# Moving token loads, first taps, one output sum and the halves of a sum in a convolution and mixture-of-experts kernel

## The chip, the core and the metric

The kernel runs on one core of one Trainium2 chip. The metric is the device time of one execution in microseconds (us), as the median over runs. Engines are named as in the profile: PE is TensorE (PEld its weight loader), DVE is VectorE, ACT is ScalarE, POOL is GpSimd, SP is SyncE, which here only issues DMAs. "L434" is line 434 of the kernel.

## The reference

Two stages follow each other. The first is a causal convolution over the sequence with seven taps, whose weights are the softmax of `weight` over the taps, one set for each of eight heads of 24 channels. The second sends each token to one of eight experts.

```python
# x (8, 3584, 192), weight (8, 7), w_gate (192, 8), w_local (192, 1),
# w1 (8, 192, 1024), w2 (8, 1024, 192), all float32
x[b, s, h, :] = sum_k softmax(weight[h])[k] * x_padded[b, s + k, h, :]      # 24 channels a head
logits = x @ w_gate
gate = sigmoid(x @ w_local)
e[b, s] = argmax(logits[b, s]) if s == 0 or gate[b, s] < 0.5 else e[b, s - 1]
p = softmax(logits[b, s])
out[b, s] = p[e] * (relu(x[b, s] @ w1[e]) @ w2[e])
```

There are 28,672 tokens.

## The kernel before

**Parts and blocks.** The tokens come in 16 parts of 1792. Each part is loaded, convolved, routed (expert, probability and a slot number for each token), and scattered row by row into slots in DRAM, where tokens of one expert stand together. The slots are then worked through in blocks of one expert each: blocks 0 to 27 hold one unit of 128 tokens, blocks 28 to 70 two units, then come 23 large blocks of four units (`FIRST` is 71, the first of them), then four blocks of two and 15 of one, and two that run only where they are needed. Routing and computing overlap: while TensorE works through blocks of tokens that are routed, the other engines convolve and route the parts that follow.

**One block** of the first 71 is: turn the tokens (`turn`, L402 on TensorE for one unit), the product with w1 (`hidden`, L1069, into four banks of PSUM named `hps`), ReLU on ScalarE (L1078), the product with w2 (`output`, L1090, into two banks named `yps`), and the output sum. The tokens' and the hidden units' halves are computed apart (64 of the 128 rows of TensorE's array each), so a result stands in two banks: ScalarE scales one of them by the probability into `o_sb` (L1100) and VectorE adds the other (L1104, the "output sum" below). This frees the two banks of `yps` for the next block. Last, GpSimd scatters the rows to the output (`deliver`, L1118).

**Convolution.** `conv(g)` works in six channel groups (`DQ`). For each, ScalarE multiplies by tap 0 (L424) and VectorE adds taps 1 to 6, one instruction each (L434, "steps" below). Only at the start of its fourth group (`b == DQ // 2`, three sixths) does it issue the load of the next part's tokens (L432, `load_x`, L150: one DMA of 1920 KB into one of two buffers). When a part is convolved, `logits` multiplies it on TensorE (L624), into the same `hps` banks, and ScalarE copies the logits out (L629).

**The order of the work** is written by hand, and every engine runs its instructions in that order. Between the pieces of a block stand calls of `step(time)`, which put so much of the convolution or of the routing into VectorE's queue: the generators yield the cost of what they issued, and `step` stops when the time is used up. In a block of one unit there are three such places: `step(2.1)` ahead of `output` (L1489; 2.4 at block 0), `step(1.2)` inside it between ScalarE's half and the output sum (L1102; nothing at block 0), and `step(1.3)` behind it (L1498). `st["block"]` is the number of the block, `TURNED` is 28, the first block of two units.

**Queues.** SyncE issues all loads, one after another: rows of a block from the slots (L990 for one unit, L998 and L1003 later; it waits there until the scatters of the group that fills them are done), the weights of a block (L982, 1536 KB, 512 KB chunks for the first few; four buffers, issued three blocks ahead) and the tokens (L150). GpSimd issues the scatters into the slots (`put`, L838). Where a route's logits are awaited (`st["due"]`), `output` issues none of them.

**Large blocks.** `seven` computes the hidden units of a block of four units with seven products in place of eight. Each product is a call of `times` (L1237, four matmuls, each of which the trace records twice), partial sums stand in three pairs of banks (`xb`, `wbk`, `yb`), and VectorE adds them to copies in SBUF: h22 takes `xb` (L1257), h11 takes `wbk` (L1259), h12 takes `yb` (L1269). Then come the ReLUs (L1261 for h11, in two halves) and `output_late` (L1287), which needs the ReLU of h11 for its weights. One matmul of the product `times(wbk, a13, b31)` is held back behind the next product:

```python
        put(times(xb, s3, t3))
        nc.vector.tensor_tensor(h22, xb, h22, op=Alu.add)       # L1257
        times(wbk, a13, b31, at=((1, 1),))
        nc.vector.tensor_tensor(h11, wbk, h11, op=Alu.add)      # L1259
```

Of the kernel before, what the change touches and what calls it, by code (L numbers as in the profile page):

```python
# [10 lines left out]
Act = mybir.ActivationFunctionType  # L11
Alu = mybir.AluOpType
# [5 lines left out]
P = 128  # L18
# [8 lines left out]
NPART = N // PT  # L27
# [19 lines left out]
EARLY = 3  # L47
# [46 lines left out]
DQ = D // Q  # L94
# [17 lines left out]
def kernel(  # L112
# [11 lines left out]
    nc = tc.nc  # L124
# [11 lines left out]
    op = ctx.enter_context(tc.tile_pool(name="op", bufs=2))  # L136
# [29 lines left out]
    c = cst.tile([P, DQ, KC], F32, name="c")  # L166
# [229 lines left out]
    def halves():  # L396
        return [(half, slice(half * DR, (half + 1) * DR)) for half in range(2)]
# [16 lines left out]
    def conv(g, x_sb):  # L414
        z = (z_tile() if g % 2 else
             ys[2].tile([P, NB, DG], F32, name="y_sb").rearrange("p b d -> p (b d)"))
        z = z[:, :NT * D].rearrange("p (b s) -> p b s", b=DQ)
        got[g] = z

        def chans(b, k):  # L420
            return x_sb[:, b, k * Q:(k + NT) * Q]

        def first(b):
            nc.scalar.activation(z[:, b, :], chans(b, 0), Act.Copy, scale=c[:, b, 0:1])  # L424

        first(0)
        yield 0
        for b in range(DQ):
            if b + 1 < DQ:
                first(b + 1)  # L430
            if b == DQ // 2 and 2 < g < NPART - 1:
                x_in[g + 1] = load_x(g + 1)  # L432
            for k in range(1, KC):
                nc.vector.scalar_tensor_tensor(z[:, b, :], chans(b, k), c[:, b, k:k + 1],  # L434
                                               z[:, b, :], Alu.mult, Alu.add)
                yield 0.68
# [389 lines left out]
    to_put = []  # L826
# [254 lines left out]
    def output(n, wb, xg, hT, w2):  # L1081

        yps = [yps_p.tile([P, 512], F32, name="yps") for half in range(2)]
        spots = {1: {(0, 0, 1): 0} if st["block"] and not st["due"] else {},
                 2: {(0, 0, 0): 0, (0, 1, 1): 2, (2, 0, 7): 0}}[n]
        for m4 in ([0, 1, 4, 5], [2, 3, 6, 7]):
            for k in range(n):
                for m in m4:
                    for half, rows in halves():
                        ins = nc.tensor.matmul(yps[half][:, k * D:(k + 1) * D],  # L1090
                                               lhsT=hT[rows, m, k * P:(k + 1) * P],
                                               rhs=wb[rows, w2 + m * D:w2 + (m + 1) * D],
                                               start=(m == 0 and k == 0), stop=(m == FK - 1),
                                               skip_group_check=True)
                    if len(to_put) > spots.get((m4[0], k, m), len(to_put)):
                        put(ins)
        o_sb = op.tile([P, KT, D], F32, name="o_sb")
        y = [[yps[half][:, k * D:(k + 1) * D] for half in range(2)] for k in range(n)]
        for k in range(n):
            nc.scalar.activation(o_sb[:, k, :], y[k][0], Act.Copy, scale=xg[:, k, 0:1])  # L1100

        step(1.2 if n > 1 or st["block"] else 0)  # L1102
        for k in range(n):
            nc.vector.scalar_tensor_tensor(o_sb[:, k, :], y[k][1], xg[:, k, 0:1], o_sb[:, k, :],  # L1104
                                           Alu.mult, Alu.add)

            st["hot"] = n == 1 and st["due"]
            if k == 0 and not st["hot"]:
                deliver(o_sb[:, 0, :], xg, 0)
            else:  # L1110
                held.append(lambda ins, k=k: deliver(o_sb[:, k, :], xg, k, ins))
# [108 lines left out]
    def seven(wb, wt, weight_then, xT, xc, rows_then, weights_next):  # L1220
# [10 lines left out]
            "p h (j s) -> p h j s", j=2)  # L1231
            for pool, name in ((late_p[0], "ps"), (xps_p, "xps"), (late_p[1], "ps"))]

        def times(to, a, b, first=False, at=((0, 0), (0, 1), (1, 0), (1, 1))):
            for j, half in at:
                rows = halves()[half][1]
                ins = nc.tensor.matmul(to[:, half, j, :], lhsT=b[rows, j * P:(j + 1) * P],  # L1237
                                       rhs=a[rows, :], start=(first and j == 0), stop=True,
                                       skip_group_check=True)
            return ins  # L1240

        weight_then(times(xb, a11, b11, True))
# [7 lines left out]
        times(xb, s2, t2)  # L1250
        nc.scalar.copy(h12, xb)
        put(times(wbk, a12, b21, True))
        times(wbk, a13, b31, at=((0, 0), (0, 1), (1, 0)))
        if st["block"] > FIRST:
            step(SIDE[0], early=1)
        put(times(xb, s3, t3))
        nc.vector.tensor_tensor(h22, xb, h22, op=Alu.add)  # L1257
        times(wbk, a13, b31, at=((1, 1),))
        nc.vector.tensor_tensor(h11, wbk, h11, op=Alu.add)  # L1259
        for side in range(2):  # L1260
            nc.scalar.activation(h11[:, side], h11[:, side], Act.Relu)  # L1261
        times(yb, s4, b22)
        put(times(yb, s5, b32))
        times(xb, a22, t4)
# [196 lines left out]
    for i, (_, n, _, _) in enumerate(blocks):  # L1461
# [15 lines left out]
        if i < FIRST:  # L1477
# [6 lines left out]
            else:  # L1484
# [1 line left out]
                xT = turn_late(n_next, xgs[i + 1][0])  # L1486
                xc = combine_x(xT)
                next(xc)
            step(2.4 if i == 0 else 2.1 if n == 1 else 4.2 if i < FIRST - 1 else 3.0)  # L1489
            xg = xgs.pop(i)  # L1490
            output(n, wbs.pop(i), xg if i < TURNED else xg[1], hT, w2)
            if i == 0:
# [2 lines left out]
                more_room()  # L1495
                xc = next(xc)
            if i < FIRST - 1:
                step(1.3 if n == 1 else 3.4)  # L1498
            continue
        if i == FIRST:  # L1500
            banks.close()
# [143 lines left out]
```

## Time and profile before

| what | value |
|---|---|
| three runs | 1310.39, 1309.5, 1309.29 us; median 1309.5 |
| the profiled execution | 1310.8 us, of which the span of instructions is 1309.0 |
| mean granted clock of TensorE | 0.993 |
| VectorE busy | 949.3 us (73%) |
| ScalarE busy | 541.3 us (41%) |
| GpSimd busy | 558.0 us (43%) |
| DMA | 299.6 MB, 229 GB/s over the span |

The share of the span says how long an engine was busy, not whether anything waited for it. A wait row gives for one engine and one kind of instruction what released it last, with the total idle time, how often, and the mean. A timeline row gives start, length, engine, line and instruction, runs of equal instructions as one with their count, and in square brackets the idle time just before with its releaser. A clock below 1.00 in a stretch means that TensorE was granted that share of full speed there. Block 2 begins its first product at 60.2 us, block 21 at 180.9, block 31 at 265.1; the first large block's products begin at 698.6 and the last one's end at about 1168 us.

### The profile page before, as it was taken

The page shows a single profiled execution, that of the slowest core. Times are in us where ns is not written, and L with a number is a line of the kernel's source. Part 1 is how long each engine was busy: PE and PEld are TensorE (multiplying, and loading weights), DVE is VectorE, ACT ScalarE, POOL GpSimd, SP SyncE. Part 2 cuts the span into 40 slices and gives each one's busy share as a digit, 9 for nine tenths or more (in the row PEclk, how much of TensorE's full clock was granted, in tenths as well). Part 3 has the DMA queues.
Part 4 walks back from the last instruction along what each step waited for, and adds up shares of the span by engine and source line. Part 5 has one row for each costly group of instructions (what it writes and reads, how often), then busy time and mean ns, then how long its engine had stood idle before and what let it go on. Part 6 is the DMA issues. An engine that isn't in the chain of part 4 may idle for free.

```text
span 1309.0 us, 39518 instructions
## 1 busy us (share of the span) xinstructions
PE 1273.4 (97%) x15406; PEld 1214.3 (93%) x15406; DVE 949.3 (73%) x2481; ACT 541.3 (41%) x1208; POOL 558.0 (43%) x619
## 2 busy tenths in 40 slices
PE   9899999899999999999999999999999999999997
PEld 7789999899999999999999998999999999999997
DVE  5978889799988989999888989976875434341111
ACT  5435554234343442434435444544434434342332
POOL 4444444344344444444545455355356433321221
PEclk9989999899999999999999999999999999999999
DMA  5789998988887878878787646464555635535894
GB/s 197 267 319 403 356 360 263 346 266 279 263 289 234 283 241 278 276 234 285 263 259 228 171 119 180 104 168 146 139 170 141 179 104 152 150 97 191 271 323 160
DMA packets 182675, 299.59 MB, mean 229 GB/s; under 512 B 145872, under 2 KB 157191, under 8 KB 166738
## 3 DMA queue, kind: packets, MB, share of 16 engines
q1 hardware_dynamic: 160160, 251.79, 60.3%
q0 software_dynamic: 22320, 45.22, 10.5%
q8 instruction: 123, 2.02, 0.6%
q14 instruction: 70, 0.57, 0.1%
q10 hardware_dynamic: 2, 0.00, 0.0%
HBM read 251.35 MB, written 46.07 MB: 227 GB/s over the span
## 4 chain that ended last, share of the span: by engine, by line
PE 89%; DVE 5%; issue 2%; ACT 2%; DMA 1%; POOL 0%; POOLq 0%; DVEq 0%; another core or an unknown queue 0%; ACTq 0%
PE hps L1069 23%; PE yps L1090 23%; PE ps L1287 22%; PE ps L1237 11%; PE ps L1182 5%; PE xps L1237 2%; PE hps L624 2%; DMA x_sb<-in_x_dram 1%; DVE z L434 1%; ACT hot L1261 1%; DVE hot L1257 1%; DVE hot L1259 1%; PE hps L252 1%; PE hps L189 0%; DVE hot L597 0%
## 5 line engine op out<-in xcount | busy, mean ns | idle before, releaser
L1118 POOL DMA_INDIRECT out_dram<-o_sb,head x201 | 208.7, 1038 | 454.1 <-DVE o_sb L1302 273.2
L1069 PE MATMUL hps<-xT,wb 64*128 64x256 f32 (+1 forms) x3408 | 323.0, 339 | 8.6 <-ACT ls L629 4.4
L1090 PE MATMUL yps<-wb,hT 64*128 64x192 f32 x3648 | 318.5, 326 | 3.9 <-DVE o_sb L1104 3.0
L1069 PEld LDWEIGHTS hps<-xT,wb 64*128 64x128 f32 x3408 | 289.0, 189 | 31.5 <-issue 6.9
L1090 PEld LDWEIGHTS yps<-wb,hT 64*128 64x128 f32 x3648 | 305.3, 188 | 7.5 <-DVE o_sb L1104 3.6
L1287 PE MATMUL ps<-wb,hot 64*128 64x192 f32 x3680 | 309.4, 324 | 3.0 <-ACT hot L1261 0.9
L1287 PEld LDWEIGHTS ps<-wb,hot 64*128 64x128 f32 x3680 | 299.3, 187 | 12.0 <-ACT hot L1261 10.6
L838 POOL DMA_INDIRECT slots<-y_sb,posi x228 | 232.9, 1022 | 175.1 <-PE yps L1090 87.3
L1078 ACT ACTIVATE hT<-hps 128x512 f32<-128x512 f32 (+1 forms) x284 | 130.6, 510 | 150.2 <-PE hps L1069 126.9
L434 DVE SCALAR_TENSOR_TENSOR y_sb<-x_sb,c,y_sb 128x448 f32<-128x448 f32 x252 | 172.7, 696 | 25.8 <-ACT y_sb L424 19.8
L434 DVE SCALAR_TENSOR_TENSOR z<-x_sb,c,z 128x448 f32<-128x448 f32 x252 | 173.1, 696 | 16.6 <-ACT z L424 8.6
L1302 DVE SCALAR_TENSOR_TENSOR o_sb<-ps,head,o_sb 128x192 f32<-128x192 f32 x115 | 43.2, 412 | 141.4 <-ACT o_sb L1297 138.7
L1297 ACT ACTIVATE o_sb<-ps,head 128x192 f32<-128x192 f32 x115 | 42.9, 417 | 204.7 <-PE ps L1287 182.9
L1100 ACT ACTIVATE o_sb<-yps,head 128x192 f32<-128x192 f32 x86 | 31.4, 417 | 159.0 <-PE yps L1090 81.9
L1237 PE MATMUL ps<-xT,wb 64*128 64x256 f32 x736 | 91.8, 376 | 0.0
L1161 DVE STREAM_TRANSPOSE xT<-y_sb 128x768 f32<-128x768 f32 (+1 forms) x65 | 54.9, 871 | 46.0 <-PE ps L1182 33.0
L1237 PEld LDWEIGHTS ps<-xT,wb 64*128 64x128 f32 x736 | 79.8, 187 | 2.1
L1257 DVE TENSOR_TENSOR hot<-ps,hot 128x1024 f32<-128x1024 f32 x23 | 28.2, 1224 | 65.1 <-PE ps L1237 49.2
L1182 PE MATMUL ps<-xT,wb 64*128 64x128 f32 (+1 forms) x912 | 64.2, 294 | 0.0
L1261 ACT ACTIVATE hot<-hot 128x512 f32<-128x512 f32 x46 | 26.5, 622 | 89.5 <-DVE hot L1259 73.4
L1182 PEld LDWEIGHTS ps<-xT,wb 64*128 64x128 f32 x912 | 62.7, 188 | 0.0
L1118 POOL DMA_INDIRECT out_dram<-o_sb,xg x28 | 30.3, 1083 | 75.6 <-DVE o_sb L1104 51.9
(296 smaller groups left out, 1439.6 us busy)
## 6 DMA issues: line engine op xcount, KB each, us to landing
wb<-in_w_dram SPq DMA_DIRECT2D x109, 1536.0 KB
x_sb<-in_x_dram SPq DMA_DIRECT2D x14, 1920.0 KB
y_sb<-slots SPq DMA_DIRECT2D x92, 192.0 KB
hot<-slots SPq DMA_DIRECT2D x172, 96.0 KB
wb<-in_w_dram SPq DMA_DIRECT2D x12, 512.0 KB
slots<-y_sb,posi POOLq DMA_INDIRECT x228
out_dram<-o_sb,head POOLq DMA_INDIRECT x201
x_sb<-in_xb_dram SPq DMA_DIRECT2D x4, 768.0 KB
```

What stands on the lines that cost most here:

```text
L434: nc.vector.scalar_tensor_tensor(z[:, b, :], chans(b, k), c[:, b, k:k + 1], z[:, b, :], Alu.mult, Alu.add)
L838: ins = nc.gpsimd.indirect_dma_start(out=slots[:, :], in_=rows, in_offset=None, out_offset=bass.IndirectOffsetOnAxis(ap=to, axis=0)).ins
L1069: ins = nc.tensor.matmul(hps[half][:, j, w], lhsT=wb[rows, w1 + f0:w1 + f0 + P], rhs=xT[rows, d, w], start=(d == 0 and j == 0), stop=(d == ...
L1078: nc.scalar.activation(hT[:, m:m + 2, w], hps[half][:, :, w], Act.Relu)
L1090: ins = nc.tensor.matmul(yps[half][:, k * D:(k + 1) * D], lhsT=hT[rows, m, k * P:(k + 1) * P], rhs=wb[rows, w2 + m * D:w2 + (m + 1) * D], ...
L1118: sent = nc.gpsimd.indirect_dma_start(out=out, in_=o, in_offset=None, out_offset=bass.IndirectOffsetOnAxis(ap=xg.bitcast(I32)[:, k, 1:2], ...
L1161: nc.vector.transpose(xT.rearrange("p d (j t) -> p j d t", t=Q)[:, js], rows[:, js].rearrange("p j (d t) -> p j d t", t=Q))
L1182: nc.tensor.matmul(hps[:, half, j, :], lhsT=wb[rows, f0:f0 + P], rhs=xT[rows, d, :], start=(d == 0 and j == 0), stop=(d == KD - 1), skip_g ...
L1237: ins = nc.tensor.matmul(to[:, half, j, :], lhsT=b[rows, j * P:(j + 1) * P], rhs=a[rows, :], start=(first and j == 0), stop=True, skip_gro ...
L1287: ins = nc.tensor.matmul(yps[:, half, k * D:(k + 1) * D], lhsT=h[two][rows, side, j, k * P:(k + 1) * P], rhs=wb[rows, f * D:(f + 1) * D], ...
L1297: nc.scalar.activation(o_sb[:, k, :], yps[:, 0, k * D:(k + 1) * D], Act.Copy, scale=xg[:, at + k, 0:1])
L1302: nc.vector.scalar_tensor_tensor(o_sb[:, k, :], yps[:, 1, k * D:(k + 1) * D], xg[:, at + k, 0:1], o_sb[:, k, :], Alu.mult, Alu.add)
```

## The change

Five edits, each an order of instructions; no instruction of arithmetic is added except that one sum of a large block becomes two of half its width.

- **Token loads at two sixths.** `conv(g)` issues the next part's load at the start of its second group of channels (`b == 1`), when the taps of one group are queued, in place of its fourth.
- **First taps follow ReLUs.** In blocks 1 to 27 a group no longer issues ScalarE's tap 0 of the group behind it ahead of its own steps; before each `step` ahead of `output`, `firsts(2)` issues tap 0 for up to two groups ahead, behind the ReLUs of that block.
- **Scatters.** `output` of a one-unit block now issues a scatter also while a route is due, if the next one in line belongs to part 3 (`EARLY`).
- **The second block's output sum.** In block 1 `step(2.1)` and `step(1.2)` become nothing and `step(1.3)` becomes `step(3.4)`: the convolution steps that stood ahead of and around its output sum go behind it.
- **One sum in two halves.** In `seven`, the sum of h11 is made in two halves of 512 columns; the first now stands ahead of the sum of h22, each half's ReLU behind it, and the product into `wbk` is no longer split.

```diff
@@ conv
-        first(0)
+        at = {"b": 0, "first": 0}
+
+        def firsts(more):
+            while at["first"] <= min(at["b"] + more, DQ - 1):
+                b = at["first"]
+                nc.scalar.activation(z[:, b, :], chans(b, 0), Act.Copy, scale=c[:, b, 0:1])
+                at["first"] += 1
+
+        st["firsts"] = firsts
+        firsts(0)
         yield 0
         for b in range(DQ):
-            if b + 1 < DQ:
-                first(b + 1)
-            if b == DQ // 2 and 2 < g < NPART - 1:
+            at["b"] = b
+            firsts(0 if 0 < st["block"] < TURNED else 1)
+            if b == 1 and 2 < g < NPART - 1:
                 x_in[g + 1] = load_x(g + 1)
@@ output
-        spots = {1: {(0, 0, 1): 0} if st["block"] and not st["due"] else {},
+        away = st["due"] and not (to_put and to_put[0][0] == EARLY)
+        spots = {1: {(0, 0, 1): 0} if st["block"] and not away else {},
@@
-        step(1.2 if n > 1 or st["block"] else 0)
+        step(1.2 if n > 1 or st["block"] > 1 else 0)
@@ seven
         put(times(wbk, a12, b21, True))
-        times(wbk, a13, b31, at=((0, 0), (0, 1), (1, 0)))
+        times(wbk, a13, b31)
         if st["block"] > FIRST:
             step(SIDE[0], early=1)
         put(times(xb, s3, t3))
-        nc.vector.tensor_tensor(h22, xb, h22, op=Alu.add)
-        times(wbk, a13, b31, at=((1, 1),))
-        nc.vector.tensor_tensor(h11, wbk, h11, op=Alu.add)
         for side in range(2):
+            nc.vector.tensor_tensor(h11[:, side], wbk[:, side], h11[:, side], op=Alu.add)
             nc.scalar.activation(h11[:, side], h11[:, side], Act.Relu)
+            if side == 0:
+                nc.vector.tensor_tensor(h22, xb, h22, op=Alu.add)
@@ the loop over blocks
-            step(2.4 if i == 0 else 2.1 if n == 1 else 4.2 if i < FIRST - 1 else 3.0)
+            if st["cgen"] and i < TURNED:
+                st["firsts"](2)
+            step((2.4, 0)[i] if i < 2 else 2.1 if n == 1 else 4.2 if i < FIRST - 1 else 3.0)
@@
-                step(1.3 if n == 1 else 3.4)
+                step(1.3 if n == 1 and i != 1 else 3.4)
```

Lines behind the first edit move down by four to eleven: steps from L434 to L440, the output sum from L1104 to L1111, weights from L982 to L988, rows from L990 to L996.

**VectorE, from the end of the early routing to block 4.** `y_sb_705` is the convolution of part 2 (the steps), `o_sb` the output of blocks 1, 2, 3 and so on (the output sums). Before:

```order
L915 CAST tabi0_2_905<-tab0_244 128x2
L918 TENSOR_TENSOR new_883<-ends0_250 128x8
L920 SCALAR_TENSOR_TENSOR used_242<-new_883,used_242 128x8
L434 SCALAR_TENSOR_TENSOR y_sb_705<-x_sb_393,c_117,y_sb_705 128x448 x8
L1104 SCALAR_TENSOR_TENSOR o_sb_991<-yps_972,xg_744,o_sb_991 128x192
L434 SCALAR_TENSOR_TENSOR y_sb_705<-x_sb_393,c_117,y_sb_705 128x448 x8
L1104 SCALAR_TENSOR_TENSOR o_sb_1083<-yps_1064,xg_795,o_sb_1083 128x192
```

And in the changed kernel:

```order
L921 CAST tabi0_2_906<-tab0_244 128x2
L924 TENSOR_TENSOR new_884<-ends0_250 128x8
L926 SCALAR_TENSOR_TENSOR used_242<-new_884,used_242 128x8
L440 SCALAR_TENSOR_TENSOR y_sb_705<-x_sb_393,c_117,y_sb_705 128x448 x2
L1111 SCALAR_TENSOR_TENSOR o_sb_988<-yps_969,xg_744,o_sb_988 128x192
L440 SCALAR_TENSOR_TENSOR y_sb_705<-x_sb_393,c_117,y_sb_705 128x448 x11
L1111 SCALAR_TENSOR_TENSOR o_sb_1079<-yps_1060,xg_795,o_sb_1079 128x192
L440 SCALAR_TENSOR_TENSOR y_sb_705<-x_sb_393,c_117,y_sb_705 128x448 x8
```

Ahead of block 1's output sum two steps stand in place of eight; ahead of block 2's stand eleven in place of eight, and block 3's keeps its eight.

**SyncE, around the rows of block 21.** `x_sb` is a token load, `wb` a block's weights, `xg` its rows. Before:

```order
L982 DMA wb_2640<-in_w12_dram 128x3072
...
L990 DMA xg_2750<-slots_113 128x195
...
L982 DMA wb_2755<-in_w12_dram 128x3072
...
L990 DMA xg_2842<-slots_113 128x195
...
L982 DMA wb_2847<-in_w12_dram 128x3072
L150 DMA x_sb_2922<-in_x_dram 128x3840
```

And in the changed kernel:

```order
L988 DMA wb_2639<-in_w12_dram 128x3072
...
L988 DMA wb_2749<-in_w12_dram 128x3072
L150 DMA x_sb_2795<-in_x_dram 128x3840
...
L996 DMA xg_2834<-slots_113 128x195
...
L996 DMA xg_2839<-slots_113 128x195
```

`wb_2755` and `wb_2749` are the weights of block 21, `xg_2750` and `xg_2834` its rows: they stood ahead of the weights, and now stand behind the weights and the tokens of part 5.

**SyncE, around the load of part 6's tokens.** `head` ends the rows of a block of two units. Before:

```order
L982 DMA wb_3626<-in_w12_dram 128x3072
...
L1003 DMA head_3726<-slots_113 128x2x2
...
L982 DMA wb_3735<-in_w12_dram 128x3072
...
L1003 DMA head_3813<-slots_113 128x2x2
...
L982 DMA wb_3822<-in_w12_dram 128x3072
L150 DMA x_sb_3861<-in_x_dram 128x3840
```

And in the changed kernel:

```order
L988 DMA wb_3627<-in_w12_dram 128x3072
L150 DMA x_sb_3721<-in_x_dram 128x3840
...
L1009 DMA head_3728<-slots_113 128x2x2
...
L988 DMA wb_3737<-in_w12_dram 128x3072
...
L1009 DMA head_3815<-slots_113 128x2x2
```

The tokens stood behind the weights of block 31 (`wb_3822`) and now stand behind those of block 29 (`wb_3626`, `wb_3627`): two blocks earlier in the queue, with the loads of blocks 30 and 31 behind them.

More of the change, by code (lines that the diff above doesn't have):

```diff
@@ L421, in chans @@
             return x_sb[:, b, k * Q:(k + NT) * Q]
-        def first(b):
-            nc.scalar.activation(z[:, b, :], chans(b, 0), Act.Copy, scale=c[:, b, 0:1])
-        first(0)
+        at = {"b": 0, "first": 0}
[6 more added lines that the diff above has]
+        firsts(0)
         yield 0
         for b in range(DQ):
-            if b + 1 < DQ:
-                first(b + 1)
-            if b == DQ // 2 and 2 < g < NPART - 1:
+            at["b"] = b
+            firsts(0 if 0 < st["block"] < TURNED else 1)
+            if b == 1 and 2 < g < NPART - 1:
                 x_in[g + 1] = load_x(g + 1)
@@ L1232, in seven, with times @@
             for pool, name in ((late_p[0], "ps"), (xps_p, "xps"), (late_p[1], "ps"))]
[L1234 to L1239, printed above, removed]
+        def times(to, a, b, first=False):
+            for j in range(2):
+                for half, rows in halves():
+                    ins = nc.tensor.matmul(to[:, half, j, :], lhsT=b[rows, j * P:(j + 1) * P],
+                                           rhs=a[rows, :], start=(first and j == 0), stop=True,
+                                           skip_group_check=True)
             return ins
```

## The prediction

> **What bounds the kernel now.** I read the page first, then the waits of TensorE and of its weight loader, then the timeline around each long wait. The page gives the frame.
>
> ```profile
> span 1309.0 us, 39518 instructions
> PE 1273.4 (97%) x15406; PEld 1214.3 (93%) x15406; DVE 949.3 (73%) x2481; ACT 541.3 (41%) x1208; POOL 558.0 (43%) x619
> PE 89%; DVE 5%; issue 2%; ACT 2%; DMA 1%; POOL 0%; POOLq 0%; DVEq 0%; another core or an unknown queue 0%; ACTq 0%
> ```
>
> TensorE is busy 1273.4 of 1309.0 us and holds 89% of the chain that ended last. The change removes none of its instructions, so all it can win lies in the 35.6 us in which TensorE is idle, and in stretches where it runs at half clock. The list of waits names the three largest that the change can reach.
>
> ```profile
> PEld ps L1287 <- ACT hot L1261: 10.6, 22, 0.6
> ...
> PE hps L1069 <- ACT ls L629: 4.4, 1, 4.4
> ...
> PE yps L1090 <- DVE o_sb L1104: 3.0, 1, 3.0
> ```
>
> Two are single stalls, one comes once in a large block. The single ones cost more than their length. In the table of stretches the columns are length, busy time of PE, PEld, DVE, ACT and POOL with counts, the granted clock, DMA share and GB/s.
>
> ```profile
> 62.10:65.50 3.40, 1.43 (x24) 1.14 (x20) 3.26 (x6) 3.23 (x10) 0.00 (x0) 1.00 1.06 417
> 65.52:72.34 6.82, 5.83 (x39) 5.83 (x41) 6.49 (x12) 0.42 (x1) 3.40 (x3) 0.50 1.00 413
> ...
> 249.80:253.20 3.40, 0.17 (x2) 0.00 (x0) 0.00 (x0) 0.26 (x1) 0.00 (x0) 1.00 1.16 265
> 253.26:260.07 6.81, 5.71 (x27) 5.71 (x29) 6.38 (x12) 2.39 (x7) 1.97 (x2) 0.50 1.11 300
> ```
>
> Behind each stall the clock is 0.50 for 6.8 us. TensorE works 5.83 and 5.71 us of these at half speed, so 2.9 us are lost each time on top of the wait.
>
> **Second block's output sum.** The timeline around the first stall (start, length, engine, line, instruction):
>
> ```profile
> 60.66 5.47 DVE L434 SCALAR_TENSOR_TENSOR y_sb<-x_sb,c,y_sb 128x448 f32<-128x448 f32 x8
> 61.64 0.42 ACT L1100 ACTIVATE o_sb<-yps,xg 128x192 f32<-128x192 f32 x1 [1.94 <-PE hps L1069]
> 62.97 0.56 PE L1090 MATMUL yps<-wb,hT 64*128 64x192 f32 x2
> 66.05 0.41 DVE L1104 SCALAR_TENSOR_TENSOR o_sb<-yps,xg,o_sb 128x192 f32<-128x192 f32 x1
> 66.37 5.60 DVE L434 SCALAR_TENSOR_TENSOR y_sb<-x_sb,c,y_sb 128x448 f32<-128x448 f32 x8
> 66.51 5.16 PE L1090 MATMUL yps<-wb,hT 64*128 64x192 f32 x29 [2.98 <-DVE o_sb L1104]
> ...
> 74.85 2.91 PE L1090 MATMUL yps<-wb,hT 64*128 64x192 f32 x30
> ```
>
> Block 1's output sum (L1104) frees the bank that block 2's output needs. It stands behind eight convolution steps of 0.684 us. After the change two stand ahead of it: they end at 60.66 + 1.37 = 62.03, ScalarE's half is there at 62.06, and the sum ends at 62.5, before TensorE asks at 62.97. The stall and its half clock go.
>
> What is late next is the sum of block 2. The order puts eleven steps ahead of it: 62.5 + 11 x 0.70 (5.60 / 8) + 0.41 = 70.6. Undisturbed, a block's two products take 2.68 and 2.66 us:
>
> ```profile
> 104.18 2.70 PE hps L1069 x48
> 107.00 2.66 PE yps L1090 x32
> ```
>
> So TensorE would ask at 62.97 + 2.66 + 2.70 + 0.1 = 68.4 and, one product on, idle for about 2.0 us, until 70.7. In the trace of before that place, block 3's output, is at 74.85. The gain is 4.1, and as block 3's sum (eight steps on, 70.6 + 5.60 + 0.41 = 76.6) is again some 0.3 late for block 4, I take 3.8. Bounds: 6.1 (stall and half clock, nothing late) and 0 (the new stall as long and as cold).
>
> The clock at this new stall is open. In the row of 62.10:65.50 an idle time of 1.97 of 3.40 us was enough for half clock behind it. My stall is as long, and whether so much of it falls into one such stretch depends on where the stretch begins. If it does, another 2.9 us go. [...]
>
> **Token loads at two sixths.** Around the second stall:
>
> ```profile
> 225.55 0.36 SPq L982 DMA_DIRECT2D wb<-in_w_dram  x1
> ...
> 237.20 0.38 SPq L150 DMA_DIRECT2D x_sb<-in_x_dram  x1
> ...
> 252.94 1.23 ACT L424 ACTIVATE y_sb<-x_sb,c 128x448 f32<-128x448 f32 x2 [6.56 <-DMA x_sb<-in_x_dram]
> ...
> 254.37 5.65 PE L1069 MATMUL hps<-xT,wb 64*128 64x256 f32 x24 [4.39 <-ACT ls L629]
> ```
>
> The chain of waits has the load itself, from issue to landing:
>
> ```profile
> 237.20 15.71 DMA x_sb<-in_x_dram
> ```
>
> ScalarE's first tap waits for the tokens; behind it in ScalarE's queue stands the copy of the logits, and TensorE waits for its banks. In the order the load moves from behind block 31's weights to behind block 29's (225.55), 11.3 us earlier. With the same 15.7 us it lands at 241.6; ScalarE asks at 252.94 - 6.56 = 246.4. So 4.8 us of margin, and the stall (4.4) and the cold stretch behind it (2.85) go, 7.2 in all. The weights of block 30, which the load now precedes, come later by one load; I take 7.0. Bounds: 7.2, and 0 if the queue holds the load up by as much as it was moved.
>
> An earlier load moves the other way. Here the row loads of block 21 and the order of SyncE meet:
>
> ```profile
> 55.00:200.00 145.00, 139.05 (x2208) 133.60 (x2207) 123.61 (x349) 74.68 (x232) 65.37 (x63) 0.98 0.92 354
> ...
> 165.00:170.00 5.00, 4.79 (x71) 4.66 (x70) 4.58 (x17) 3.27 (x10) 2.02 (x3) 1.00 0.36 119
> ```
>
> ```profile
> 158.43 0.33 SPq L982 DMA_DIRECT2D wb<-in_w_dram  x1
> 168.14 0.01 SPq L990 DMA_DIRECT2D xg<-slots  x1
> 168.91 0.33 SPq L982 DMA_DIRECT2D wb<-in_w_dram  x1
> ```
>
> ```profile
> 178.13 0.22 PE L402 MATMUL xps<-ident,xg 64*128 64x64 f32 x1
> ```
>
> Before, SyncE waits until 168.14 for the scatters of that group, then fetches block 21's rows, then its weights. After, weights and tokens go ahead of the rows, from about 164, when the buffer is free. At 354 GB/s weights (1536 KB) and tokens (1920 KB) take 4.4 + 5.6 us: the rows land near 178, when TensorE wants to turn them (178.13). Against that stands the stretch at 119 GB/s, where the queue had room. I book a loss of 0.7; bounds 0 and 5.6 (all of the token load). [...]
>
> The ten later loads move the same bytes into stages where TensorE waits for no transfer: nothing.
>
> **First taps behind ReLUs; scatters.** In the one-unit blocks ScalarE's taps no longer stand ahead of the ReLUs. What TensorE waited there:
>
> ```profile
> PE yps L1090 <- ACT hT L1078: 0.3, 1, 0.3
> ```
>
> I take 0.3; bounds 0.9 and -0.7 (one tap of 0.66 us in front of a copy that frees a bank). The scatters that now go while a route is due shift by one block on GpSimd, 43% busy: nothing.
>
> **Large blocks.** One block's end (timeline):
>
> ```profile
> 1042.41 1.23 DVE L1257 TENSOR_TENSOR hot<-ps,hot 128x1024 f32<-128x1024 f32 x1 [4.59 <-PE ps L1237]
> ...
> 1043.55 1.22 DVE L1259 TENSOR_TENSOR hot<-xps,hot 128x1024 f32<-128x1024 f32 x1
> ...
> 1044.68 1.22 DVE L1269 TENSOR_TENSOR hot<-ps,hot 128x1024 f32<-128x1024 f32 x1
> ...
> 1046.02 10.40 PEld L1287 LDWEIGHTS ps<-wb,hot 64*128 64x128 f32 x128 [0.46 <-ACT hot L1261]
> 1046.05 10.67 PE L1287 MATMUL ps<-wb,hot 64*128 64x192 f32 x128
> ```
>
> Three sums run back to back on VectorE; the third, which frees the bank of the output, ends at 1045.90, and the weight load starts at 1046.02. A load usually leads its product by about 0.2 us (here 0.03), so of the 0.46 some 0.25 reach TensorE. After the change half of the second sum runs ahead of the first, in VectorE's 4.59 us of idle time. A half costs about 0.70 by the nearest row of that width:
>
> ```profile
> L597 DVE TENSOR_TENSOR hot<-rel,wb 112x512 f32<-112x512 f32 x8 | 5.1, 695 | 0.0
> ```
>
> The third sum then starts about 0.4 earlier (1.22 + 0.70 in place of 2 x 1.22, and it now waits for its product), and the output goes straight on. VectorE is free at that place in 20 of 23 blocks:
>
> ```profile
> DVE hot L1257 <- PE ps L1237: 49.2, 14, 4.6
> ...
> DVE hot L1257 <- PE xps L1237: 15.7, 6, 4.0
> ```
>
> 20 x 0.25 = 5.0, less 0.1 in each of the other three, where the half delays the rest: 4.7. Bounds: 9.2 (20 x 0.46) and -3.
>
> **Sum.** 3.8 + 7.0 - 0.7 + 0.3 + 4.7 = 15.1 us. The profiled execution took 1310.8 (span 1309.0 and 1.8 around it): 1295.7. The median of the runs shown is 1.3 lower: 1294.4.
>
> **Rivals.** (1) The new stall at block 3 brings half clock again: 2.9 less, 1297.3. For it: 1.97 us of idle time were enough before. Against: it needs the stall to lie in one stretch. (2) The half sums bring nothing, because the half that now stands first delays the sum behind it and with it the next product: 4.7 less, 1299.1. The half can begin when the second sum's matmuls are done, and four others (one product) then run before the sum behind it can begin. In the chain 32 records, two to a matmul, took 3.45 us, so four matmuls take 0.9; the rival holds if a half costs more, and the 0.70 speaks against it.
>
> ```profile
> 1036.28 3.45 PE ps L1237 x32
> ```
>
> (3) The token load doesn't land in time after all and half of the 7.0 stays: 1297.9; the margin of 4.8 us speaks against it. (4) Slower: the token load ahead of rows and weights in SyncE's one queue stops TensorE in the early stage. Three loads move there (the ones that serve parts 4, 5 and 6). If each holds its next block up for all of its 5.6 us and leaves a cold stretch of 2.9, 25.5 us go and 1294.4 becomes 1319.2, less the 0.7 booked. It is slower than before from (15.1 + 0.7 + 2.6) / 3 = 6.1 us a place on. Against it: no wait of TensorE before names a transfer, and weights are issued three blocks ahead.
>
> **How the numbers follow.** Chances: forecast 0.45, (1) 0.28, (2) 0.12, (3) 0.10, (4) 0.05. The range goes from 1289.5 (no loss at block 21, all of 6.1 in block 2) to 1301.5, which takes in (1), (2), (3) and (1) with (2). Three runs spread by 1.1 us, so 0.2% or 2.6 us is about what can be told from no change; faster means under 1306.9. Only (4), or several losses together, leaves that: faster 0.94, same 0.03, slower 0.03.
>
> **What would show it.** Right: no wait of L1090 in block 2, one of about 2 us in block 3; no wait of ScalarE for tokens near 246, and full clock from there; the loader's waits at the large blocks' output gone, the stretch from one large block's output to the next shorter by 0.25; at most a short wait when block 21's rows are turned. Wrong: half clock after 68, a longer period of the large blocks, or TensorE waiting for rows or weights between 110 and 260.

## The result and the profile after

The changed kernel takes 0.9906 of the time before (95% interval 0.9891 to 0.9920): 12.3 us less on the 1309.5 us of the first runs (10.5 to 14.3), where 15.1 were forecast. The medians are 1299.7 and 1313.3 us, of 18 runs each. The profiled execution took 1300.1 us, with a span of 1298.3, 10.7 us under that of before.

```profile
span 1298.3 us, 39551 instructions
PE 1263.3 (97%) x15406; PEld 1206.5 (93%) x15406; DVE 952.3 (73%) x2504; ACT 545.5 (42%) x1208; POOL 558.1 (43%) x619
```

The waits of TensorE, and of its weight loader at the large blocks' output (the third figure of a wait row is the longest wait, not the mean):

```profile
PE xps L402 <- DMA xg<-slots: 2.7, 1, 2.7
PE yps L1097 <- DVE o_sb L1111: 2.7, 4, 1.3
...
PEld ps L1294 <- issue: 2.5, 6, 0.7
```

The stalls of 4.4 and 3.0 us and the loader's 10.6 us are gone. In their place stand a wait for rows, 2.7 us at one block, and four short ones for an output sum. Where the time went shows when the starts of blocks are set side by side (first row of L1069, now L1075, of a block in the timeline; us from one to the next). The second pair of columns is from two later executions, side by side on one chip, of the kernel before and of the changed one. Single executions differ by some us: in five later ones with the large blocks of the change, the last stretch took 625.6 to 631.3 us.

```
stretch                    before   after   less    before   after   less   forecast
start to block 4            77.54   73.44    4.1     75.27   73.31    2.0    3.8
block 4 to 28              147.14  153.91   -6.8    147.00  150.56   -3.6   -0.4
block 28 to 31              40.38   33.28    7.1     40.30   32.97    7.3    7.0
block 31 to 69             410.45  411.07   -0.6    411.61  411.23    0.4    0
block 69 to the end        633.49  626.60    6.9    635.22  625.63    9.6    4.7
span                      1309.0  1298.3    10.7   1309.4  1293.7   15.7   15.1
```

The two edits that were to gain most did so, the large blocks gained more than forecast, and the stretch from block 4 to 28 gave much of it back.

**Block 2 and 3.** The timeline of the changed kernel (start, length, engine, line, instruction; idle time before it in brackets):

```profile
61.01 1.27 DVE L440 SCALAR_TENSOR_TENSOR y_sb<-x_sb,c,y_sb 128x448 f32<-128x448 f32 x2
62.12 0.42 ACT L1107 ACTIVATE o_sb<-yps,xg 128x192 f32<-128x192 f32 x1
62.57 0.42 DVE L1111 SCALAR_TENSOR_TENSOR o_sb<-yps,xg,o_sb 128x192 f32<-128x192 f32 x1 [0.29 <-ACT o_sb L1107]
...
69.18 0.54 PE L1097 MATMUL yps<-wb,hT 64*128 64x192 f32 x2
...
70.58 0.41 DVE L1111 SCALAR_TENSOR_TENSOR o_sb<-yps,xg,o_sb 128x192 f32<-128x192 f32 x1
70.91 5.60 DVE L440 SCALAR_TENSOR_TENSOR y_sb<-x_sb,c,y_sb 128x448 f32<-128x448 f32 x8
71.05 2.70 PE L1097 MATMUL yps<-wb,hT 64*128 64x192 f32 x29 [1.33 <-DVE o_sb L1111]
```

Block 1's sum ends at 62.99, and block 2's output goes on without a wait. Block 2's sum, behind eleven steps, ends at 70.99 and stops TensorE for 1.33 us.

**The load of part 6's tokens** is issued at 228.36, and where TensorE stood for 4.39 us the logits are now followed at once by the next block at full clock (windows: length, busy time of PE, PEld, DVE, ACT and POOL, clock, DMA share, GB/s):

```profile
246.00:254.40 8.40, 8.33 (x166) 7.22 (x164) 8.15 (x14) 3.36 (x8) 2.63 (x4) 1.00 1.10 333
```

**The rows of block 21.** SyncE's DMAs, GpSimd's scatters and the turning of the rows:

```profile
164.14 1.30 SPq L150 DMA_DIRECT2D x_sb<-in_x_dram  x1
166.20 1.15 POOL L844 DMA_INDIRECT slots<-y_sb,posi  x1 [0.71 <-PE yps L1097]
...
175.01 1.25 SPq L996 DMA_DIRECT2D xg<-slots  x2
...
179.29 0.34 PE L402 MATMUL xps<-ident,xg 64*128 64x64 f32 x4 [2.74 <-DMA xg<-slots]
```

The scatter at 166.20 is the last of part 2, which SyncE waits for ahead of these rows. Before, the last one was issued at 164.01 and the rows at 168.14, in time:

```profile
164.01 0.96 POOL L838 DMA_INDIRECT slots<-y_sb,posi  x1 [0.30 <-issue]
168.14 0.01 SPq L990 DMA_DIRECT2D xg<-slots  x1
```

Now the rows are issued at 175.01 and TensorE has them at 179.29, 2.74 us late.

**Large blocks.** VectorE's three sums and the output:

```profile
1034.27 0.69 DVE L1265 TENSOR_TENSOR hot<-xps,hot 128x512 f32<-128x512 f32 x1 [3.74 <-PE xps L1244]
...
1035.13 1.23 DVE L1268 TENSOR_TENSOR hot<-ps,hot 128x1024 f32<-128x1024 f32 x1 [0.17 <-PE ps L1244]
1036.27 0.68 DVE L1265 TENSOR_TENSOR hot<-xps,hot 128x512 f32<-128x512 f32 x1
...
1036.87 1.22 DVE L1276 TENSOR_TENSOR hot<-ps,hot 128x1024 f32<-128x1024 f32 x1
...
1038.30 1.01 PE L1294 MATMUL ps<-wb,hot 64*128 64x192 f32 x10
...
1058.22 0.49 PE L1294 MATMUL ps<-wb,hot 64*128 64x192 f32 x3
```

The first half (0.69 us, forecast 0.70) is done before the sum of h22 begins, and the output no longer waits. From one output to the next it is 19.92 us, against 20.44 before (from 1046.05 to the next output, in the chain of the kernel before): 0.52 less, where 0.25 was forecast.

```profile
1066.48 10.67 PE ps L1287 x128
```

### The profile page after: what moved, and what is told of

Read it like the earlier page. It is cut to its first block, busy times and chain, and to the rows that moved or that the text cites. A ratio compares the mean times of both kernels' runs of the same rounds, so it can differ in the third digit from the quotient of the medians.

```text
span 1298.3 us, 39551 instructions
## 1 busy us (share of the span) xinstructions
PE 1263.3 (97%) x15406; PEld 1206.5 (93%) x15406; DVE 952.3 (73%) x2504; ACT 545.5 (42%) x1208; POOL 558.1 (43%) x619
## 3 DMA queue, kind: packets, MB, share of 16 engines
q0 software_dynamic: 22320, 45.22, 10.7%
## 5 line engine op out<-in xcount | busy, mean ns | idle before, releaser
L1075 PE MATMUL hps<-xT,wb 64*128 64x256 f32 (+1 forms) x3408 | 317.7, 337 | 4.7 <-issue 3.2
L1097 PEld LDWEIGHTS yps<-wb,hT 64*128 64x128 f32 x3648 | 301.6, 187 | 8.9 <-DVE o_sb L1111 3.9
L1075 PEld LDWEIGHTS hps<-xT,wb 64*128 64x128 f32 x3408 | 281.1, 187 | 30.7 <-issue 8.0
L440 DVE SCALAR_TENSOR_TENSOR y_sb<-x_sb,c,y_sb 128x448 f32<-128x448 f32 x252 | 172.7, 695 | 21.9 <-ACT y_sb L428 15.8
L440 DVE SCALAR_TENSOR_TENSOR z<-x_sb,c,z 128x448 f32<-128x448 f32 x252 | 172.8, 695 | 20.8 <-ACT z L428 11.6
L1107 ACT ACTIVATE o_sb<-yps,head 128x192 f32<-128x192 f32 x86 | 31.5, 417 | 155.6 <-PE yps L1097 79.8
L1244 PE MATMUL ps<-xT,wb 64*128 64x256 f32 x736 | 88.6, 376 | 1.1 <-DVE xT L1220 1.1
L1265 DVE TENSOR_TENSOR hot<-xps,hot 128x512 f32<-128x512 f32 x46 | 31.5, 685 | 44.7 <-PE xps L1244 44.6
```

The source lines that it names most:

```text
L1075: ins = nc.tensor.matmul(hps[half][:, j, w], lhsT=wb[rows, w1 + f0:w1 + f0 + P], rhs=xT[rows, d, w], start=(d == 0 and j == 0), stop=(d == ...
L1097: ins = nc.tensor.matmul(yps[half][:, k * D:(k + 1) * D], lhsT=hT[rows, m, k * P:(k + 1) * P], rhs=wb[rows, w2 + m * D:w2 + (m + 1) * D], ...
```

## The experiments

### One edit at a time

Four kernels, each the kernel before with one edit, ran on one chip, on which the kernel before takes 1294.8 us. The theory was that the parts add up and that each loses where the traces say.

**The output sum alone:**

```diff
-        step(1.2 if n > 1 or st["block"] else 0)
+        step(1.2 if n > 1 or st["block"] > 1 else 0)
-            step(2.4 if i == 0 else 2.1 if n == 1 else 4.2 if i < FIRST - 1 else 3.0)
+            step((2.4, 0)[i] if i < 2 else 2.1 if n == 1 else 4.2 if i < FIRST - 1 else 3.0)
-                step(1.3 if n == 1 else 3.4)
+                step(1.3 if n == 1 and i != 1 else 3.4)
```

> Only the second block's output sum is moved (steps of block 1 behind it); all else as before. Theory (the parts add, and each loses where the two traces say): the stall of 2.98 us in block 2 and its half clock go, a stall of 1.3 us comes in block 3 at full clock, so block 4 begins some 4 us earlier (before: 77.54). The last scatter of part 2 falls one block later, so SyncE waits for it until about 175 us and the rows of block 21 come late: a wait of TensorE for a transfer near 177 us, 1 to 2 us long here, where no token load stands ahead of the rows. The stall of 4.4 us near 250 stays. Whole: 2 to 4 us faster. Rival (the token load alone made the rows late): no wait for a transfer near 177; whole: 4 us faster or more.

Measured: 1.0033 (1.0021 to 1.0045), 4.3 us slower. From block 2 to block 4 it takes 11.52 us, where the other three kernels of this chip take 15.6 to 15.7, so the gain of 4 us is there. It is given back by block 28, which begins at 220.3, against 214.8 to 215.3 in the others. The longest waits of TensorE:

```profile
PE hps L1069 <- ACT ls L629: 4.4, 1, 4.4
PE xps L402 <- DMA xg<-slots: 3.4, 3, 2.8
PE hps L624 <- issue: 2.0, 1, 2.0
```

The stall near block 30 stays. For rows near blocks 21 and 22 TensorE waits 0.4 us in one place, not the 1 to 2 forecast; the 2.8 us lie in block 1, and the 2.0 in the logits at 187, behind which the mean granted clock was 0.75 from 189.4 to 196.2 us. How much of these two is the edit's and how much chance, one trace can't tell. The timed runs say that this edit, alone, costs more than it gains. The theory's "2 to 4 us faster" falls, and the rival's 4 with it.

**The token loads alone** (`if b == 1` for `if b == DQ // 2`):

> Only the token loads are issued at two sixths. Theory: the stall of 4.4 us near 250 us and the half clock behind it go, 7.2 us in all; the rows of block 21 stand ahead of its weights and of the token load here, since no scatter has moved, so no wait for a transfer near 180. The stall of block 2 stays. Whole: about 7 us faster. Rival (the token load alone makes rows late): a wait of 2 to 3 us for rows near 180 to 187, whole about 4 us faster.

Measured: 0.9956 (0.9942 to 0.9971), 5.7 us faster. From block 30 to 31 it takes 10.49 us, where the kernels with the old loads take 15.6, 16.4 and 17.9 on this chip. There is no wait for rows near 180, so the load alone doesn't make them late, and the rival falls.

**The first taps and the scatter rule alone:**

> Only the first taps follow the ReLUs and the scatter rule for part 3 is changed. Theory (the first taps, issued later on ScalarE, make VectorE late): VectorE's waits for first taps get longer, an output sum is late somewhere in blocks 4 to 27, and block 28 begins 1 to 2 us later than before (224.68). Both stalls of before stay. Whole: 1 to 2 us slower. Rival (the forecast): 0.3 us faster; the losses in blocks 4 to 27 of the changed kernel then come from the other edits.

Measured: 0.9981 (0.9968 to 0.9994), 2.5 us faster. The theory falls: block 28 begins at 215.25, within 0.5 us of the two kernels beside it without this edit. The stall near block 30 is 3.3 us in place of 4.1:

```profile
PE hps L1075 <- ACT ls L635: 3.3, 1, 3.3
```

That is 0.8 us; the rest of the 2.5 couldn't be placed in the trace. The rival's 0.3 is too little as well.

**The halves alone:**

> Only the large blocks are changed: h11's sum in two halves and the product into wbk not split. Theory (two gains: the bubble of 0.25 us ahead of the output, and 0.2 more, since the split product left TensorE's two halves of rows out of step by one matmul): an undisturbed large block takes 19.9 us in place of 20.44, the 23 blocks together 7 to 11 us less. Rival (the bubble alone, as forecast): 20.2 us a block, about 5 us less. All up to the first large block as before.

Measured: 0.9942 (0.9928 to 0.9957), 7.5 us faster. One output to the next, in a stretch of undisturbed blocks:

```profile
1121.49 0.36 PE L1287 MATMUL ps<-wb,hot 64*128 64x192 f32 x2
...
1141.41 0.36 PE L1287 MATMUL ps<-wb,hot 64*128 64x192 f32 x2
```

19.92 us: the theory's size, not the rival's 20.2. The four alone give 4.3 - 5.7 - 2.5 - 7.5 = -11.4 us (0.9912), close to the changed kernel's 0.9906: the parts add up, and one of them is a loss.

### The place of the steps

The next four kernels ran on another chip (before: 1313.2 us), among them the kernel before and the changed one once more.

> The kernel before once more, on the chip of the three kernels beside it, for its trace there. As in the first trace: a stall of about 3 us in block 2 with lower clock behind it, one of about 4 us near block 30, large blocks of 20.44 us.

```profile
64.00:67.20 3.20, 0.24 (x3) 0.15 (x4) 3.13 (x6) 1.87 (x6) 0.00 (x0) 1.00 1.03 421
67.20:74.00 6.80, 6.80 (x98) 6.58 (x100) 6.55 (x11) 2.52 (x8) 4.29 (x4) 1.00 1.01 394
```

The stall in block 2 is there again, 2.96 us, but the clock behind it stays at 1.00 this time. Near block 30 the stall was 5.2 us.

> The changed kernel once more, beside its traces. Theory (the new order of the steps in block 1 lets part 2's route begin one block later, and with it every scatter up to block 20): 10 to 13 us faster than before; from the start of block 4 to that of block 28 it takes 4 us or more longer than before, with SyncE waiting at the rows of block 21 and TensorE behind it. Rival (the loss between blocks 4 and 28 was chance in one execution): those blocks take as long as before, and the whole is 14 us faster or more.

Measured: 0.9912 (0.9896 to 0.9927). Blocks 4 to 28 take 150.56 us against 147.00, so 3.6 us longer, and SyncE issues the rows of block 21 at 174.92; TensorE waits 1.1 us for them. The loss comes again, but its size varies (6.8 in the first pair).

The theory on the cause: behind the early routing part 2's convolution has 25 steps left. In eights a block the 25th stands behind block 3's sum, so that block 4's first call begins the route. With two, eleven and eight ahead of the first three sums, four are left for block 4, the route begins later, and the scatters of part 2 end one block later. A kernel that moves the sums and keeps eight steps a block tells it apart:

```diff
-        step(1.2 if n > 1 or st["block"] > 1 else 0)
+        step(1.2 if n > 1 or st["block"] > 3 else 0)
-            step((2.4, 0)[i] if i < 2 else 2.1 if n == 1 else 4.2 if i < FIRST - 1 else 3.0)
+            step((2.4, 0, 0, 0)[i] if i < 4 else 2.1 if n == 1 else 4.2 if i < FIRST - 1 else 3.0)
-                step(1.3 if n == 1 and i != 1 else 3.4)
+                step((5.0 if 0 < i < 4 else 1.3) if n == 1 else 3.4)
```

> The changed kernel, but in blocks 1, 2 and 3 all steps stand behind the output sum, eight in each block as before (two, eight, eight, seven ahead of the sums of blocks 1 to 4, in place of two, eleven, eight, four). So part 2's route and its scatters keep the places that they had before, and the rows of block 21 stand ahead of its weights again. Theory: no wait of TensorE for an output sum in blocks 2 and 3, none above 0.5 us for rows at block 21; 17 to 21 us faster than before (5.7, 2.5 and 7.5 for the other three edits as measured alone, and 4 to 5 for the sums), so 6 us or more faster than the changed kernel. Rival (moving the sums costs by itself, whatever the place of the scatters): no faster than the kernel with the sums as before, which runs beside it.

Measured: 0.9860 (0.9842 to 0.9878), 18.4 us faster than before and the best version of this study. The sums of blocks 2 and 3:

```profile
68.30 0.41 DVE L1111 SCALAR_TENSOR_TENSOR o_sb<-yps,xg,o_sb 128x192 f32<-128x192 f32 x1
68.62 5.60 DVE L440 SCALAR_TENSOR_TENSOR y_sb<-x_sb,c,y_sb 128x448 f32<-128x448 f32 x8
68.78 2.85 PE L1097 MATMUL yps<-wb,hT 64*128 64x192 f32 x32
...
74.14 0.41 DVE L1111 SCALAR_TENSOR_TENSOR o_sb<-yps,xg,o_sb 128x192 f32<-128x192 f32 x1
...
74.85 2.85 PE L1097 MATMUL yps<-wb,hT 64*128 64x192 f32 x32
```

Block 2's sum ends at 68.71, just ahead of the output that starts at 68.78, and neither output waits; the rows of block 21 come in time. The next limit shows too: TensorE, now 3.8 us ahead at block 4, meets the rows of block 7 before their scatters are done.

```profile
89.20 1.48 SPq L996 DMA_DIRECT2D xg<-slots  x2
...
91.42 0.33 PE L402 MATMUL xps<-ident,xg 64*128 64x64 f32 x4 [2.20 <-DMA xg<-slots]
```

The same with the sum's move taken out, the other edits in:

> The changed kernel with the steps of block 1 as before: token loads, first taps and halves are in, the output sum's move is out. Theory (the parts add): 15 to 16 us faster than before (5.7 and 2.5 and 7.5 as measured alone), so 4 us faster than the changed kernel; the stall in block 2 is back, the wait at block 21 is not there. Rival (the four edits need one another): slower than the changed kernel by the 4 us of the stall and its half clock.

Measured: 0.9901 (0.9883 to 0.9919), 13.0 us faster, a little under the theory's 15 to 16; the stall in block 2 is back (2.6 us), no wait at block 21. The move of the sum as the change made it is worth nothing that can be told (0.9912 with it; alone, on the other chip, it lost 4.3 us). Moving the sums of blocks 1 to 3 with eight steps a block is worth 5.4 us (0.9860 against 0.9901), and those two intervals don't overlap. The rival (moving sums costs by itself) falls. But not all of the loss behind block 4 is the late scatters': blocks 4 to 28 take 150.51 us here too, 3.5 more than in the kernel before, with the scatters in their old places; with the three sums they take 148.72.

### The load beside the late scatters

The changed kernel with the load of part 5 back at three sixths:

```diff
-            if b == 1 and 2 < g < NPART - 1:
+            if b == (DQ // 2 if g == 4 else 1) and 2 < g < NPART - 1:
```

> The changed kernel with one load alone put back: the tokens of part 5 are issued at three sixths again, behind the weights of block 22, so that the rows of blocks 21 and 22 stand ahead of them; the scatters still fall one block late. Theory (late scatters and the token load make the wait at block 21 together; each alone was hidden): the rows of block 21 are issued near 175 us as in the changed kernel and land within 2 us, TensorE waits for them under 0.5 us in place of 1.1 to 2.7; whole 11 to 14 us faster than before. Rival (the late scatters alone): the wait stays at 1 us or more.

Measured: 0.9903 (0.9889 to 0.9917), 12.7 us. SyncE, and the turning of the rows of blocks 21 and 23:

```profile
172.97 1.26 SPq L996 DMA_DIRECT2D xg<-slots  x2
...
175.21 0.42 SPq L150 DMA_DIRECT2D x_sb<-in_x_dram  x1
...
175.52 0.29 PE L402 MATMUL xps<-ident,xg 64*128 64x64 f32 x3
...
176.68 0.02 SPq L996 DMA_DIRECT2D xg<-slots  x1
...
188.79 0.33 PE L402 MATMUL xps<-ident,xg 64*128 64x64 f32 x4 [1.57 <-DMA xg<-slots]
```

The rows of block 21 come in time, so the wait there is made by both together, as the theory says. (They are issued at 172.97, 2 us sooner than in the changed kernel.) But the load only moved the wait: the rows of block 23, issued behind it, come 1.57 us late. With the rows a block late, something behind the load waited at both places tried. The rows issued ahead of the load were in use 2.6 us later, those behind it 12.1.

### The split product

Two kernels take the large blocks' edit apart. The changed kernel with the split product back (its last matmul between the two half sums):

> The changed kernel with the product into wbk split again as before, its last matmul behind the next product, while the sums stay in halves. Theory (two gains of about equal size: the wait ahead of the output, and TensorE's two halves of rows in step): an undisturbed large block takes 20.13 us, 0.21 more than the 19.92 of the changed kernel, with no bubble ahead of the output. Rival (the halves alone gave it all): 19.92.

The theory's size was wrong. From one output to the next:

```profile
1042.82 0.40 PE L1295 MATMUL ps<-wb,hot 64*128 64x192 f32 x1
...
1063.32 0.56 PE L1295 MATMUL ps<-wb,hot 64*128 64x192 f32 x3
```

20.50 us, 0.58 more than the changed kernel, with nothing idle ahead of the output. Besides one matmul's slot, the held-back matmul itself waited: its first record started 0.37 us behind the one before it, its second 0.32 behind that, in place of 0.216. The loader's waits name the first half sum, behind which the matmul stands in the program:

```profile
PEld xps L1244 <- DVE hot L1265: 10.2, 21, 2.1
```

It writes the bank of the other half, which that sum doesn't read; why it waits all the same isn't shown. The halves need the whole product.

The kernel before with the whole product and the old sums:

> The kernel before, with the product into wbk whole, and the sums as before (h22 first, then h11 in one piece). Theory: the three sums one behind the other still set the start of the output, so the time that the whole product saves only makes the bubble ahead of the output longer: 20.4 us a large block, bubble about 0.45. Rival (the split alone cost it): 20.2 us or less.

```profile
PEld ps L1286 <- ACT hot L1260: 14.6, 23, 0.6
...
1068.31 0.43 PE L1286 MATMUL ps<-wb,hot 64*128 64x192 f32 x2 [0.26 <-ACT hot L1260]
```

As the theory said: 20.45 us a block. The matmuls save one slot, and the output waits that much longer for the sums (0.68 us from the last matmul's start to the output's, 0.46 before). Each half of this edit alone brings nothing; together they bring 0.52 us a block. (One execution of each was timed: 1309.3 us with the halves kept, 1317.2 us with the old sums, beside 1312.3 for the kernel before.)

### The first taps once more

The kernel with the three sums, with the taps as before:

```diff
-            firsts(0 if 0 < st["block"] < TURNED else 1)
+            firsts(1)
-            if st["cgen"] and i < TURNED:
-                st["firsts"](2)
```

> The kernel with the sums of blocks 1 to 3 ahead of the steps (1.4% faster than before when it ran), with the first taps issued as before: one group ahead, at the start of each group. Theory (the first taps in pairs behind the ReLUs gain little and cost little): within 3 us of that kernel, so 15 to 21 us faster than before; TensorE's waits for a ReLU in blocks 20 to 27 (0.3 to 0.6 us) go, VectorE's waits for taps get no longer. Rival (the taps' place is worth the 2.5 us that it gave alone): 15.5 us or less.

Measured: 0.9898 (0.9882 to 0.9914), 13.4 us faster, 5 us behind the kernel with the taps behind the ReLUs (0.9860, timed earlier on this chip). The rival holds. A tap ahead of the ReLUs delays the second half of an output:

```profile
PE yps L1097 <- ACT hT L1084: 2.1, 5, 0.5
```

Three of these five waits, 0.35 us each, lie in blocks 2 to 4, where the other kernel has none. They don't make up the 5 us; the two traces differ by 2.3 us.

## Why the prediction was right in sum, and which steps failed

**The second block's sum** (3.8): the mechanism and the size were right, 4.1 us at block 4 in the first pair. Block 1's sum ends at 62.99 (62.5 forecast), block 2's at 70.99 (70.6). TensorE asked later than forecast, at 69.18 and not 68.4, since block 2 began at 60.63 and took 5.76 us, so that the new stall is 1.33 us and not 2.0. In the second pair the gain is 2.0, since the half clock behind the old stall, which the term counts at 2.9, did not come there.

**The step that failed** is "The scatters that now go while a route is due shift by one block on GpSimd, 43% busy: nothing.", and with it the 168.14 of the token-load term, the moment at which the scatters for block 21 are done, which the forecast took over from before. It is not that rule that shifts them: with the first taps and the rule alone, block 20 takes 5.72 us. The sum's move does, by the steps that it deals out otherwise, and for this the forecast has no term. GpSimd had the time, but the last scatter of part 2 is what SyncE's row loads wait for. One block later there, and the rows of block 21, which the forecast had booked at a loss of 0.7 us for the token load alone, cost 3.3 in the first pair and 1.25 in the second (block 20 to 21: 9.04 for 5.74, 7.33 for 6.07). The late route also meets block 6's sum, for which block 7's output waits: 0.69 and 0.70 us in the two traces of the changed kernel, and not at all with eight steps a block. Leaving out the chip of the single edits, blocks 4 to 8 take 33.5 us in the four executions with the shift, and 31.5 to 32.0 in five of the six without it (the sixth, with the three sums, has the wait of 2.20 us for block 7's rows). The two places make 4.9 of the 6.8 us and 3.3 of the 3.6. That the shift, and not the move of the sum, makes these waits is shown by the kernel with the three sums, which has neither. What the rest of the stretch owes to it stays open, since the kernel without the sum's move loses 3.5 us there without a late scatter.

**The token loads** (7.0): right. 7.1 and 7.3 us from block 28 to 31, 5.7 (3.8 to 7.5) alone. ScalarE no longer waits for the tokens.

**First taps** (0.3): too little, by the timed 2.5 us (0.8 to 4.1) and the 5 us between two kernels with the three sums. The traces place under 2 us of it.

**Large blocks** (4.7): the mechanism was right and the term too small: 6.9 and 9.6 us in the traces, 7.5 (5.6 to 9.3) alone. Missing was the split itself. A product's two halves of rows run side by side, two records to a slot of 0.216 us (1044.07 to 1045.37 in the trace of before). Before, the odd matmul put the halves out of step: one slot at the split and the last one before the output held one record each, a slot in all. With the bubble (0.245) that makes 0.46 of the 0.52. Such a slot counts as busy: TensorE's busy time fell by 10.1 us, of which the two stretches at half clock make 5.8, so the frame that all the gain lies in idle time and in stretches at half clock was too narrow.

**The rivals.** The forecast's sum takes full clock at the new stall, which no trace of before shows. Half clock did not come there: the clock is 1.00 from 66 to 73.4 us.

```profile
66.00:73.40 7.40, 6.07 (x90) 5.77 (x88) 7.11 (x12) 3.95 (x13) 2.77 (x3) 1.00 1.02 412
```

The halves brought something, and the load of part 6 landed in time. The slower rival came in small, at one of its three places, and needed the late scatter for it.

**That the sum came near is in part luck.** Measured alone, the loads, the taps and the halves gained 15.7 us where 12.0 were forecast, and the sum's move lost 4.3 where 3.1 (3.8 - 0.7) were to be gained: two errors that partly cancel.

**The working.** Three numbers don't follow from what is named for them. No loss at block 21 and all of 6.1 in block 2 give 1291.4, not 1289.5; (1) with (2) gives 1302.0, just beyond 1301.5; and 164 + 4.4 + 5.6 is 174, not 178, so by those figures the rows would have come in time.

## What to carry to other kernels

A step that is moved takes along what its generator starts next: ask not only which instruction is late now, but at which call the next route, scatter or load begins, and who waits for the last of them. Where the work is dealt out in portions, move an instruction without changing how many portions are dealt by each point. The kernel that did so, and moved two more sums, was 6.8 us faster than the change (0.9860 against 0.9912 on one chip); the two traces place 3.7 of it, 1.9 up to block 4 and 1.8 from there to block 28. Two edits that each bring nothing can bring much together when one shortens an engine's work and the other the wait that hides it.

## What the runs showed of the hardware

**The same stall brought half clock in some executions and not in others.** The stall in block 2 in two of them, the kernel without the sum's move and that with the loads alone (busy times and clock in the stall, and behind it):

```profile
64.00:66.60 2.60, 0.05 (x1) 0.00 (x0) 2.53 (x6) 1.87 (x6) 0.00 (x0) 1.00 1.02 413
67.20:70.60 3.40, 3.40 (x26) 3.40 (x26) 3.29 (x5) 0.00 (x0) 2.79 (x3) 0.52 1.04 418
```

```profile
62.50:65.30 2.80, 0.01 (x1) 0.01 (x2) 2.73 (x6) 1.81 (x6) 0.00 (x0) 1.00 1.06 423
66.80:70.00 3.20, 3.20 (x27) 3.20 (x25) 3.09 (x5) 0.42 (x1) 2.23 (x2) 0.50 1.03 425
```

These two (2.56 and 2.80 us idle) ran at half clock for about 3.4 us behind it, the first execution of before (2.98) for 6.8, and the second one of before (2.96) and the changed kernel behind its 2.74 us at block 21 not at all. Of the 3.4 us ahead of the drop 1.97 were idle in the first trace of before, 2.56 and 2.08 in the two quoted here. The drop begins 1.0 us ahead of the stall's end in the first of them (65.5), 0.7 and 1.3 behind it in the two quoted here: at no fixed distance.

The times of the drops may say why. In the first trace of before the clock falls at 65.52 and 253.25 us and is back at 1.00 at 72.34 and 260.08: 6.83, 180.91 and 6.83 us apart, which is 2, 53 and 2 times 3.413. In the second trace of before it falls at 249.83; 54 times 3.413 us ahead of that lies 65.51, in the middle of the stall:

```profile
62.10:65.51 3.41, 1.99 (x31) 1.69 (x28) 3.23 (x6) 3.25 (x11) 0.00 (x0) 1.00 1.06 420
65.51:68.93 3.42, 1.88 (x22) 1.89 (x24) 3.35 (x6) 0.42 (x1) 1.36 (x2) 1.00 1.03 422
68.93:72.34 3.41, 3.41 (x61) 3.41 (x59) 3.27 (x6) 0.94 (x3) 2.05 (x2) 1.00 0.98 406
```

1.42 and 1.54 us are idle in the stretches on both sides of 65.51, and the clock stayed at 1.00; ahead of the three drops 1.97 to 2.56 us were idle. That the clock behind the stall depends on how such stretches divide it is the author's estimate from these four traces. Half clock lasted 3.4 us in the two rows quoted first, with no idle time in them, and 6.8 us in the first trace of before (65.52 to 72.34), with 0.99 us idle.

**How soon SyncE is let go behind a scatter varies.** It was let go 4.1 us behind the issue of part 2's last scatter before (164.01 to 168.14), 8.8 and 9.1 us in the two traces of the changed kernel (166.20 to 175.01, 165.80 to 174.92), and still 7.6 us with the load of part 5 put back (165.35 to 172.97). So the tokens in flight aren't all of it; what is, the runs don't show.

**Chips differ by more than the change.** The kernel before took 1294.8 us on one chip and 1312 to 1313 on another, so each ratio here is to runs of the kernel before on the same chip.
